# Copying a convolution out of PSUM earlier, and six narrow leading blocks in place of four, in a convolution + GELU MLP kernel

## Chip, cores, metric

One core of one Trainium2 chip. The metric is device time in microseconds (us), lower is better. The granted TensorE clock (the share of full speed that TensorE was given, 1.000 being all of it) is listed where it matters.

## The reference

`x` is [8, 4096, 192] fp32. A causal depthwise convolution of 7 taps (softmax-normalised weights, one set per group of 24 channels) feeds a two-layer MLP with exact GELU, 192 -> 2048 -> 192, over 32768 tokens:

```python
w = softmax(weight)                                   # [8, 7]
out[b, s, h, g] = sum_k w[h, k] * x_pad[b, s + k, h, g]   # 6 zeros ahead of each sequence
h = out @ w_in                                        # [32768, 2048]
y = (0.5 * h * (1 + erf(h / sqrt(2)))) @ w_out        # [32768, 192]
```

## The kernel before

Tokens go in blocks; each block holds a stretch of tokens of the first half of the batch on 64 partitions and the same stretch of the second half on the other 64. Per block, VectorE transposes x and does the convolution (21 operations: 7 taps for each of 3 channel groups), TensorE does the up-projection slice by slice into `hp` (PSUM), ScalarE does the GELU from `hp` to `gT`, and TensorE does the down projection of the block before, interleaved, into `ob` (PSUM), from where it is copied to `osb` and stored.

The first two blocks are an exception: TensorE does their convolution, with diagonal matrices. Their result sits in `ob` and is copied to `xc`, from where the up-projection reads it. For block 0 ScalarE copies, for block 1 VectorE (`conv_out`). Blocks are counted from 0: the third block is block 2.

```python
WS = [256] * 4 + [512] * ((HALF - 1024) // 512)   # block widths
PC = {0: 0, 1: 1}                                 # blocks whose convolution TensorE does
NA = 4                                            # blocks whose output ScalarE copies out of PSUM
...
def conv_out(n, p):                               # VectorE, L396
    v.wait_ge(S_PC, pce(n, p))                    # TensorE's convolution of group p is done
    b, o = CONVB[n][p]
    v.tensor_copy(xc[n % 2][:, p * TB : p * TB + WS[n]], ap(b, o, [[1024, 128], [1, WS[n]]])
    ).then_inc(S_PCE)
...
# VectorE's order for a block: 3 transposes (0-2), then 21 convolution steps (3-23).
# `side` puts other work ahead of a position: (block, position).
side = [((2, (4, 9, 14)[p]), conv_out, 1, p) for p in range(NP)]
for n in range(4, NB): ...                        # output copies (evac) of blocks 4.. by VectorE
...
# TensorE: block 1's up-projection waits for conv_out's S_PCE, then its first down projection
if n == 1 and a0 == 0 and a1 > 0:
    t.wait_ge(S_WOUT, 16)                         # w_out has landed
```

A slice of up-projection with its share of down projection takes TensorE 1.31 us and its GELU takes ScalarE 1.02 us, so in the steady state TensorE is the bound.

## Time and profile before

| | before |
|---|---|
| time, first three executions | 694.42, 694.45, 695.52 us |
| profiled execution | 695.67 us, span 693.8 us, granted clock 0.998 |
| busy in the span | PE 684.3, VectorE 554.3, ScalarE 531.4, GpSimd 44.6 us |
| TensorE idle | 9.5 us, nearly all before 30 us and after the last block |

In the profile's lines PE is TensorE (PEld its weight loads), DVE VectorE, ACT ScalarE, POOL GpSimd and SP SyncE. The span (first to last instruction) is 1.8 us shorter than the time of the same execution; times are compared with times and spans with spans. PE is 99% busy, so a change can gain only where TensorE stands still or runs at a lower clock. The prediction shows the lines.

### The profile page before, as it was taken

How to read it: one execution, taken by the hardware profiler on the slowest of the kernel's cores; microseconds unless marked ns; L12 is line 12 of the kernel's file. 1: busy time of each engine (PE TensorE's matmuls, PEld its weight loads, DVE VectorE, ACT ScalarE, POOL GpSimd, SP SyncE). 2: the span in 40 equal slices, each digit the busy share in tenths (PEclk: the TensorE clock that was granted, in tenths of full speed). 3: DMA queues.
4: the chain of work that ended last, by engine and by line, in shares of the span. 5: the costliest groups of instructions: out<-in, count | busy, mean ns of one | idle time of the engine just before them, and what ended most of it. 6: DMA issues, size and time to landing. Idle time of an engine off the chain costs nothing.

```text
span 693.8 us, 25405 instructions
## 1 busy us (share of the span) xinstructions
PE 684.3 (99%) x11556; PEld 502.5 (72%) x11556; DVE 554.3 (80%) x922; ACT 531.4 (77%) x532; POOL 44.6 (6%) x95
## 2 busy tenths in 40 slices
PE   8899999999999999999999999999999999999997
PEld 5696677777777777777777777777777777777777
DVE  6999677789777789778888777898877898777811
ACT  6589877777777777777777777777777777777771
POOL 7100000000000000000000000000000000000000
PEclk9999999999999999999999999999999999999999
DMA  9778453355543355543355543355543455521013
GB/s 200 161 167 186 104 119 87 85 124 138 138 112 87 90 126 137 138 105 89 88 132 137 138 101 86 90 138 137 135 99 78 102 138 137 134 50 33 17 47 94
DMA packets 23083, 78.16 MB, mean 113 GB/s; under 512 B 6976, under 2 KB 11200, under 8 KB 19136
## 3 DMA queue, kind: packets, MB, share of 16 engines
q1 hardware_dynamic: 18448, 72.26, 44.4%
q0 software_dynamic: 3792, 3.50, 2.9%
q8 instruction: 91, 1.49, 1.0%
q10 hardware_dynamic: 736, 0.78, 0.4%
q14 instruction: 16, 0.13, 0.1%
HBM read 52.92 MB, written 25.17 MB: 113 GB/s over the span
## 4 chain that ended last, share of the span: by engine, by line
PE 95%; DMA 2%; ACT 1%; DVE 1%; POOL 1%; issue 0%
PE ob L647 48%; PE hp L615 46%; DMA xin<-in_x_dram 2%; ACT gT L547 1%; DVE acc L443 0%; POOL xin L204 0%; DVE xT L413 0%; DVE acc L436 0%; POOL xTb L302 0%; ACT osb L194 0%; ACT L496 0%; DVE xc L396 0%; DVE osb L196 0%
## 5 line engine op out<-in xcount | busy, mean ns | idle before, releaser
L547 ACT ACTIVATE gT<-hp 128x1024 bf16<-128x1024 f32 x512 | 523.4, 1024 | 144.0 <-PE hp L615 144.0
L647 PEld LDWEIGHTS ob<-wout,gT 64*128 64x128 bf16 x8192 | 353.1, 94 | 115.2 <-PE ob L647 0.6
L647 PE MATMUL ob<-wout,gT 64*128 64x192 bf16 x8192 | 421.2, 243 | 0.1
L615 PE MATMUL hp<-xc,win 64*128 64x512 bf16 (+1 forms) x3264 | 416.7, 364 | 4.3 <-DVE xc L396 3.3
L443 DVE SCALAR_TENSOR_TENSOR acc<-xT,wcol,acc 128x512 f32<-128x512 f32 (+1 forms) x480 | 316.8, 722 | 0.0
L615 PEld LDWEIGHTS hp<-xc,win 64*128 64x128 bf16 x3264 | 150.3, 94 | 66.2 <-ACT gT L547 3.7
L196 DVE COPY osb<-ob 128x384 f32<-128x384 f32 x120 | 65.8, 548 | 128.8 <-PE ob L647 128.8
L443 DVE SCALAR_TENSOR_TENSOR xc<-xT,wcol,acc 128x512 bf16<-128x512 f32 (+1 forms) x96 | 64.5, 722 | 0.0
L413 DVE STREAM_TRANSPOSE xT<-xin 128x512 f32<-128x512 f32 (+1 forms) x102 | 61.0, 649 | 3.8 <-issue 2.1
L308 POOL COPY xT<-xT 128x558 f32<-128x558 f32 x32 | 20.9, 654 | 587.9 <-DVE xT L413 587.9
L436 DVE TENSOR_SCALAR acc<-xT,wcol 128x512 f32<-128x512 f32 (+1 forms) x96 | 55.4, 629 | 1.1
L291 POOL COPY xT<-xT 128x18 f32<-128x18 f32 x29 | 11.6, 398 | 4.9 <-DVE xc L396 4.9
L560 PE MATMUL hp<-warm 128*128 128x512 bf16 x16 | 6.0, 559 | 1.3 <-DVE warm L328 1.3
L576 PE MATMUL ob<-xTb,dg 64*64 64x256 bf16 x84 | 5.3, 271 | 0.3 <-ACT xTb L510 0.2
L560 PEld LDWEIGHTS hp<-warm 128*128 128x128 bf16 x16 | 2.1, 137 | 4.7 <-issue 3.2
L576 PEld LDWEIGHTS ob<-xTb,dg 64*64 64x64 bf16 x84 | 4.3, 107 | 1.5 <-ACT xTb L510 0.7
L204 POOL DMA_DIRECT2D xin<-in_x_dram x10 | 5.1, 514 | 0.0
L258 POOL DMA_DIRECT2D win<-in_moe_w_in_dram x6 | 3.9, 657 | 0.0
L194 ACT ACTIVATE osb<-ob 128x384 f32<-128x384 f32 x8 | 3.9, 484 | 0.0
L373 DVE COPY win<-win 64x768 bf16<-64x768 bf16 (+1 forms) x6 | 3.2, 526 | 0.3
L510 ACT ACTIVATE xTb<-xT 128x256 bf16<-128x256 f32 x3 | 1.1, 417 | 2.7 <-DVE xT L413 2.7
L302 POOL CAST xTb<-xT 128x186 bf16<-128x186 f32 x6 | 2.4, 404 | 2.4 <-DVE xT L413 2.4
(29 smaller groups left out, 14.1 us busy)
## 6 DMA issues: line engine op xcount, KB each, us to landing
xin<-in_x_dram SPq DMA_DIRECT2D x120, 380.0 KB, 6.6
out_dram<-osb SPq DMA_DIRECT2D x116, 192.0 KB, 3.1
out_dram<-osb SPq DMA_DIRECT2D x40, 48.0 KB, 1.9
xin<-in_x_dram POOLq DMA_DIRECT2D x10, 188.0 KB, 5.8
wout<-in_moe_w_out_dram POOLq DMA_DIRECT2D x1, 768.0 KB, 10.2
xin<-in_x_dram SPq DMA_DIRECT2D x4, 188.0 KB, 4.1
win<-in_moe_w_in_dram POOLq DMA_DIRECT2D x4, 96.0 KB, 4.3
win<-in_moe_w_in_dram POOLq DMA_DIRECT2D x2, 192.0 KB, 4.8
```

The lines of the kernel that those rows point to most:

```text
L196: e.tensor_copy(dst, src).then_inc(S_EV)
L204: e.dma_start(ap(xin[n % NX], 32 * q * (TB // 32 * D), [[TB // 32 * D, 32], [1, mb * D - 32]],), ap(xt, off, [[mb * D, 32], [1, mb * D - 3 ...
L291: g.tensor_copy(dst, ap(xT[(n - 1) % 2], WS[n - 1] + 31, [[NP * XW, 128], [XW, NP], [32, HB]],),).then_inc(S_HALO)
L308: g.tensor_copy(ap(t, 1, [[NP * tw, 128], [tw, NP], [32, HB], [1, 31]]), ap(t, WS[n], [[NP * tw, 128], [tw, NP], [32, HB], [1, 31]]),).the ...
L413: v.transpose(ap(xT[n % 2], p * XW + HL, [[NP * XW, 128], [1, w]]), ap(xin[n % NX], 64 * p, [[TB // 32 * D, 128], [D, w // 32], [1, 32]],) ...
L436: ins = v.tensor_scalar(a, src, wk, None, ALU.mult)
L443: ins = v.scalar_tensor_tensor(dst, src, wk, a, op0=ALU.mult, op1=ALU.add)
L547: a.activation(out=ap(gT[n % 2], i * c * 2 * w, dst), in_=ap(hp[u % 2], 0, src), func=AF.Gelu,).then_inc(S_GELU)
L560: t.matmul(hp[1][:, 0:512], warm[:, 0:128], warm[:, :])
L576: ins = t.matmul(b[r, o : o + w], dg[r, d0 : d0 + 64], xTb[PC[n]][r, x0 : x0 + w], start=(k == KS - 1), stop=(k == 0), tile_position=(64 * ...
L615: ins = t.matmul(hp[u % 2][:, hf * TB + cc * w : hf * TB + cc * w + w], win[r, p * F + wcols(hf, f0) : p * F + wcols(hf, f0) + 128], xc[n ...
L647: ins = t.matmul(ob[gg % 2][:, 512 * sub : 512 * sub + C], gT[m % 2][r, c0 : c0 + 128], wout[r, CH[i] * C : (CH[i] + 1) * C], start=(ph == ...
```

## The change

The intent: block 1's convolution should leave PSUM before block 2's transposes and most of block 2's convolution steps get in its way, and VectorE, pressed harder early on, should get easier early blocks. So the three copies move from positions 4, 9, 14 of block 2 to 0, 3, 5; and two more narrow blocks lead, whose outputs ScalarE copies.

```diff
-    WS = [256] * 4 + [512] * ((HALF - 1024) // 512)
+    WS = [256] * 6 + [512] * ((HALF - 1536) // 512)
-    NA = 4
+    NA = 6
-            side = [((2, (4, 9, 14)[p]), conv_out, 1, p) for p in range(NP)]
+            side = [((2, (0, 3, 5)[p]), conv_out, 1, p) for p in range(NP)]
-            for n in range(4, NB):
+            for n in range(NA, NB):
```

The first copy thus precedes block 2's transposes (position 0), the second follows them directly (3), the third comes two convolution steps later (5).

## The prediction

> **What bounds the kernel now.** I read the page first, then the waits between 16 and 30 us, the timeline of the first 110 us, and last the table of windows. The chain that ended last says which engine sets the end:

> ```profile
> ## 4 chain that ended last, share of the span: by engine, by line
> PE 95%; DMA 2%; ACT 1%; DVE 1%; POOL 1%; issue 0%
> ```

> TensorE carries 95% of the chain, and from 30 us to the last block it is 100% busy in every window. So nothing done for another engine after 30 us can gain anything; only an idle TensorE can give time back, and it idles in the first 30 us. The waits of 16 to 30 us name where (total us, times, longest us):

> ```profile
> PE hp L615 <- DVE xc L396: 3.3, 2, 1.8
> DVE xT L413 <- DMA xin<-in_x_dram: 1.5, 1, 1.5
> ```

> L396 is exactly what the change moves: VectorE copying block 1's convolution, which TensorE made in PSUM, to `xc`. The timeline (start us, duration us, engine, line) shows how late that copy is:

> ```profile
> 15.04 0.95 PE L576 MATMUL ob<-xTb,dg 64*64 64x256 bf16 x14
> 16.68 0.95 PE L576 MATMUL ob<-xTb,dg 64*64 64x256 bf16 x14
> 17.03 1.10 DVE L413 STREAM_TRANSPOSE xT<-xin 128x256 f32<-128x256 f32 x3 [1.51 <-DMA xin<-in_x_dram]
> 18.33 0.95 PE L576 MATMUL ob<-xTb,dg 64*64 64x256 bf16 x14
> 18.91 0.41 DVE L396 CAST xc<-ob 128x256 bf16<-128x256 f32 x1
> 19.21 0.83 PE L615 MATMUL hp<-xc,win 64*128 64x256 bf16 x12
> 20.95 0.41 DVE L396 CAST xc<-ob 128x256 bf16<-128x256 f32 x1
> 21.51 0.39 PE L615 MATMUL hp<-xc,win 64*128 64x256 bf16 x4 [1.47 <-DVE xc L396]
> 23.26 0.41 DVE L396 CAST xc<-ob 128x256 bf16<-128x256 f32 x1
> 23.73 1.03 PE L615 MATMUL hp<-xc,win 64*128 64x256 bf16 x8 [1.83 <-DVE xc L396]
> 25.52 1.35 PE L615 MATMUL hp<-xc,win 64*128 64x256 bf16 x12
> 27.37 0.81 PE L615 MATMUL hp<-xc,win 64*128 64x256 bf16 x12
> ```

> The three convolution parts are ready where the L576 groups end, at 16.0, 17.65 and 19.3 us, but copied at 18.91, 20.95 and 23.26, because the copies stand among block 2's convolution steps. TensorE, free at 20.04, stalls twice. It pays again afterwards (window; span; busy us of PE, PEld, DVE, ACT, POOL; granted clock; DMA share; GB/s):

> ```profile
> 9.53:12.95 3.42, 2.80 (x44) 1.62 (x39) 1.86 (x4) 2.33 (x4) 3.33 (x6) 1.00 1.04 243
> 19.77:23.19 3.42, 0.66 (x10) 0.14 (x4) 3.42 (x10) 1.02 (x1) 0.00 (x0) 1.00 0.74 185
> 23.19:26.60 3.41, 2.87 (x32) 2.22 (x34) 3.41 (x10) 1.02 (x1) 0.41 (x1) 0.50 0.59 150
> ```

> After a stretch with 0.66 us of work in 3.42 the clock is granted at 0.50 for the next 3.41 us. Stretches with 2.80 us of work did not cost it.

> [...] the first 256-wide TENSOR_SCALAR of block 2 took 0.83 us beside a GpSimd copy where its neighbours took 0.30. [...]

> **The change part by part.**

> *Move of the copies.* The first goes ahead of the transposes: ready at 16.0, it runs at about 16.05 to 16.46, inside the 1.51 us that VectorE waits for x until 17.03. It costs nothing. The second goes after the three transposes, 18.15 to 18.56 (ready 17.65). Then two TENSOR_SCALARs, one stretched by GpSimd (0.83 + 0.30), and the third copy at about 19.7 to 20.1 (ready 19.3). TensorE is free at 20.04, reaches the third part about 0.2 us later, and so does not stall. Block 1's first up-projection slice (12 matmuls, 0.65 us at full clock) ends near 20.7.

> *The next wait.* TensorE then waits for `w_out`:

> ```profile
> 11.38 1.21 POOL L317 DMA_DIRECT2D wout<-in_moe_w_out_dram  x1
> wout<-in_moe_w_out_dram POOLq DMA_DIRECT2D x1, 768.0 KB, 10.2
> ```

> 11.38 + 10.2 = 21.6 us. Before, that was hidden behind the late copies; now TensorE idles from 20.7 to 21.65. [...] Then 12 matmuls of the down projection (half of the 0.96 us that they took at half clock: 0.50), a slice of up-projection (0.65), 16 matmuls (0.66), and the third slice starts at 21.70 + 0.50 + 0.65 + 0.66 = 23.5, where before it started at 27.53 on the chain. Gain here: 4.0 us. The stalls give 3.3 - 0.95 = 2.35 of it, the clock about 1.6.

> *Six blocks of 256.* Two 256-blocks take the place of one 512-block; the work is the same. A slice with its share of down projection takes 1.315 us in 256-blocks (36.72 to 55.13 in 14 slices), 1.307 in 512-blocks: 16 slices x 0.008 = 0.13 us lost. ScalarE gets 4 more evictions at 0.48 us; 8 GELUs at 1.02 plus 2 x 0.48 = 9.1 us per block, against TensorE's 10.5, so nothing shows. The passage from the last 256-block to the first 512-block, where ScalarE sets the pace (16 GELUs in 15.95 us for TensorE's 15.7), moves from block 4 to block 6 and costs the same.

> Sum: 4.0 - 0.13 = about 3.85 us gained against the profiled execution.

> **Can VectorE keep up when TensorE is 4 us ahead?** This is what the second part is for. Before, block 4 and 5's convolutions end and block 4's first matmul comes at:

> ```profile
> 50.59 2.07 DVE L443 SCALAR_TENSOR_TENSOR xc<-xT,wcol,acc 128x512 bf16<-128x512 f32 x3
> 56.94 0.81 PE L615 MATMUL hp<-xc,win 64*128 64x512 bf16 x6
> 66.11 2.07 DVE L443 SCALAR_TENSOR_TENSOR xc<-xT,wcol,acc 128x512 bf16<-128x512 f32 x3
> ```

> With TensorE at 53.0 there, a 512-wide block 4 ready at 52.3 would have 0.7 us in hand. With 256-blocks VectorE needs 9.5 us per block against 10.5: block 2, ready at 27.63 before, loses its first copy (0.41) from the sequence and is ready at about 27.2; blocks 3, 4, 5 at 36.7, 46.2, 55.7. They are wanted at 32.0, 42.5, 53.0, 63.5 (36.06 - 4.0, and 10.5 more each). The first 512-block (15.6 us) is ready at 71.3 and wanted at 74.0: 2.7 us in hand. Block 7: 86.9 against 90.0. Old block 6, which starts at the same token as new block 7, began at 93.8; 93.8 - 90.0 = 3.8 confirms the sum. From there on TensorE is the bound as now.

> **Rivals.** (1) `w_out` lands later. By the landing records in the trace 15 of its 16 parts are there by 20.7 us and the last at 21.6, so the arrival is not firm; every us later costs one, and at 2 us later the clock could fall too (another 1.5), for 693 to 694. Against it: nothing that loads before it changes. Were it in time, the limit is another 0.95 us of gain: 690. (2) The 2.7 us at block 6 is used up, because the loads of x, queued behind stores, come late, or VectorE is slowed by GpSimd. Its load, 2.6 us after block 3 began before (49.16 against 46.6), would be issued near 45.1 and land by 52 (6.6 us in the page), wanted at 55.7; so against. Were it so, 1 to 2 us return: 693. (3) The timed executions don't hold the half-clock stretch. The profiled execution took 695.67 us, timed ones 694.42, 694.45 and 695.52. The 1.1 us between the two groups is close to the clock's 1.6[...], so the median may already be without it. Then the gain against the median is about 4.0 - 0.13 - 1.1 = 2.7, for 691.7; if profiling merely adds a us, it is 3.85, for 690.6.

> **Range and chances.** I weigh the two readings of (3) about 60 to 40 and add a little for (1): 691.4 us, which is 3 us or 0.44% less. Low end 690.2 (full gain, earlier `w_out`), high end 692.7 (`w_out` a us late). A change of 2% is 13.9 us; TensorE's idle time in the whole span is 693.8 - 684.3 = 9.5, so faster by 2% is next to impossible, and slower needs a stall that no view suggests: 0.01 each.

> **What would show it.** In the new profile: the three copies at L396 at about 16.1, 18.2 and 19.7 us; no wait of `hp` on `xc` there, but an idle TensorE of about 1 us ending near 21.6; granted clock 1.00 from 20 to 30 us; the third slice of block 1 near 23.5; block 6's first 512-wide matmul near 74 without a wait on VectorE; span near 690. I am wrong if the clock still falls to 0.50, if TensorE waits for VectorE at block 6, or if the copies stretch well beyond 0.41 us.

The sum came to 4.0 - 0.13 = about 3.85 us against the profiled execution. But about 1.6 of the 4.0 supposes that the clock stays at 1.00, and that was the author's guess. So is the fall of the clock if `w_out` came 2 us later, by likeness to the stretch with 0.66 us of work in 3.42.

## The result, and the profile after

The changed kernel took 692.07 us (median of 4, 691.64 to 692.22), the kernel before 694.91 (median of 4, 694.42 to 695.52): ratio 0.9958, 95% interval 0.994 to 0.9975. In a later session of five rounds it was 0.9945 (0.9933 to 0.9958). So: within 2%, and faster by about half a per cent.

The waits of the changed kernel between 10 and 30 us (total us, times, longest). No line has `hp` waiting on VectorE's copy to `xc` (L396) any more; this stands in its place:

```profile
PE ob L647 <- DMA wout<-in_moe_w_out_dram: 1.1, 1, 1.1
```

The timeline of the changed kernel (start us, duration us, engine, line):

```profile
16.27 0.42 DVE L396 CAST xc<-ob 128x256 bf16<-128x256 f32 x1 [0.51 <-PE ob L576]
17.08 1.10 DVE L413 STREAM_TRANSPOSE xT<-xin 128x256 f32<-128x256 f32 x3 [0.39 <-DMA xin<-in_x_dram]
18.10 0.39 DVE L396 CAST xc<-ob 128x256 bf16<-128x256 f32 x1
19.45 1.48 PE L615 MATMUL hp<-xc,win 64*128 64x256 bf16 x24
19.56 0.42 DVE L396 CAST xc<-ob 128x256 bf16<-128x256 f32 x1 [0.26 <-PE ob L576]
22.00 0.67 PE L647 MATMUL ob<-wout,gT 64*128 64x192 bf16 x12 [1.07 <-DMA wout<-in_moe_w_out_dram]
22.50 0.82 PE L615 MATMUL hp<-xc,win 64*128 64x256 bf16 x12
23.82 0.82 PE L615 MATMUL hp<-xc,win 64*128 64x256 bf16 x12
```

The first copy now fills part of VectorE's wait for x. The 24 matmuls from 19.45 on are block 0's last slice and block 1's first, in one piece: the two stalls of 1.47 and 1.83 us are gone. TensorE then stands for 1.07 us until `w_out` has landed. In the chain of the changed kernel, which is read as what released what, that load now covers the stretch where before the transposes, VectorE's convolution steps and its copies stood:

```profile
8.61 3.01 POOL xin L204 x6
11.62 10.33 DMA wout<-in_moe_w_out_dram
22.00 0.67 PE ob L647 x12
```

The windows of the changed kernel (span; busy us of PE, PEld, DVE, ACT, POOL; granted clock; DMA share; GB/s), around the wait for `w_out`; they are cut at whole multiples of 3.413 us after this execution's first clock record (4.98 us), the spacing of the clock's changes that e3 gives:

```profile
18.63:22.04 3.41, 2.34 (x41) 1.75 (x42) 3.15 (x9) 2.75 (x3) 0.54 (x2) 1.00 1.28 256
22.04:25.46 3.42, 3.35 (x70) 2.99 (x72) 3.42 (x10) 2.02 (x3) 0.00 (x0) 1.00 0.32 68
```

With 2.34 us of work in 3.41 the clock was kept: 1.00 in both. The third slice of block 1 starts at 23.82 where before, in the same view, it started at 27.37: 3.55 us gained. The lead is kept to the end almost whole: the last stretch of down projection starts at 675.48 instead of 678.91.

### The profile page after: what moved, and what is told of

It is laid out like the page before. It is cut to its first block, busy times and chain, and to the rows that moved or that the text cites. A ratio compares the mean times of both kernels' runs of the same rounds, so it can differ in the third digit from the quotient of the medians. Undisturbed runs are those within 1.5% of the kernel's fastest.

```text
span 690.5 us, 25644 instructions
## 1 busy us (share of the span) xinstructions
PE 682.3 (99%) x11652; PEld 506.3 (73%) x11652; DVE 555.7 (80%) x942; ACT 532.0 (77%) x536; POOL 45.1 (7%) x97
## 4 chain that ended last, share of the span: by engine, by line
PE 95%; DMA 2%; ACT 1%; POOL 1%; issue 0%; DVE 0%
PE ob L647 48%; PE hp L615 46%; DMA wout<-in_moe_w_out_dram 1%; ACT gT L547 1%; DMA xin<-in_x_dram 1%; POOL xin L204 0%; POOL xTb L302 0%; ACT osb L194 0%; ACT L496 0%; DVE osb L196 0%; DVE xT L413 0%
## 5 line engine op out<-in xcount | busy, mean ns | idle before, releaser
L615 PE MATMUL hp<-xc,win 64*128 64x512 bf16 (+1 forms) x3360 | 415.5, 358 | 1.0 <-ACT gT L547 0.7
L443 DVE SCALAR_TENSOR_TENSOR acc<-xT,wcol,acc 128x512 f32<-128x512 f32 (+1 forms) x495 | 318.7, 710 | 0.0
L615 PEld LDWEIGHTS hp<-xc,win 64*128 64x128 bf16 x3360 | 154.6, 94 | 61.0 <-ACT gT L547 1.9
L196 DVE COPY osb<-ob 128x384 f32<-128x384 f32 x116 | 63.9, 551 | 124.2 <-PE ob L647 124.2
L443 DVE SCALAR_TENSOR_TENSOR xc<-xT,wcol,acc 128x512 bf16<-128x512 f32 (+1 forms) x99 | 65.1, 713 | 0.0
L413 DVE STREAM_TRANSPOSE xT<-xin 128x512 f32<-128x512 f32 (+1 forms) x105 | 61.3, 635 | 2.9 <-issue 2.1
L308 POOL COPY xT<-xT 128x558 f32<-128x558 f32 x33 | 21.5, 652 | 587.5 <-DVE xT L413 587.5
L576 PE MATMUL ob<-xTb,dg 64*64 64x256 bf16 x84 | 5.3, 271 | 1.1 <-ACT xTb L510 1.0
L576 PEld LDWEIGHTS ob<-xTb,dg 64*64 64x64 bf16 x84 | 4.3, 106 | 2.3 <-ACT xTb L510 1.5
L194 ACT ACTIVATE osb<-ob 128x384 f32<-128x384 f32 x12 | 5.8, 486 | 0.0
## 6 DMA issues: line engine op xcount, KB each, us to landing
wout<-in_moe_w_out_dram POOLq DMA_DIRECT2D x1, 768.0 KB, 10.3
```

Source lines behind the costliest of these rows:

```text
L194: e.activation(out=dst, in_=src, func=AF.Copy).then_inc(S_EVA)
L196: e.tensor_copy(dst, src).then_inc(S_EV)
L308: g.tensor_copy(ap(t, 1, [[NP * tw, 128], [tw, NP], [32, HB], [1, 31]]), ap(t, WS[n], [[NP * tw, 128], [tw, NP], [32, HB], [1, 31]]),).the ...
L413: v.transpose(ap(xT[n % 2], p * XW + HL, [[NP * XW, 128], [1, w]]), ap(xin[n % NX], 64 * p, [[TB // 32 * D, 128], [D, w // 32], [1, 32]],) ...
L443: ins = v.scalar_tensor_tensor(dst, src, wk, a, op0=ALU.mult, op1=ALU.add)
L576: ins = t.matmul(b[r, o : o + w], dg[r, d0 : d0 + 64], xTb[PC[n]][r, x0 : x0 + w], start=(k == KS - 1), stop=(k == 0), tile_position=(64 * ...
```

## The experiments

Eleven runs, all correct: nine new kernels, the changed kernel again (e5) and e8 again (e11). Those of one table ran on one chip in the same rounds, five or six executions each.

| first session | median us | ratio to before, 95% | granted clock |
|---|---|---|---|
| before (11 runs) | 695.85 | 1 | 0.995 to 1.000 |
| e1 copies moved, four blocks | 692.20 | 0.9948 (0.9935 to 0.9962) | 0.999 to 1.000 |
| e2 six blocks, copies late | 695.64 | 1.0000 (0.9984 to 1.0016) | 0.995 to 1.000 |
| e3 before, stalls filled | 694.88 | 0.9988 (0.9974 to 1.0002) | 0.999 to 1.000 |
| e4 changed, block 3's x after `w_out` | 690.93 | 0.9932 (0.9918 to 0.9945) | 0.999 to 1.000 |

**e1, the moved copies alone.** Edit, against the kernel before:

```diff
-            side = [((2, (4, 9, 14)[p]), conv_out, 1, p) for p in range(NP)]
+            side = [((2, (0, 3, 5)[p]), conv_out, 1, p) for p in range(NP)]
```

> Only the earlier copies, four 256-blocks as before. My theory: the whole gain is made before 30 us, so this keeps it and loses nothing to the extra 256-blocks: 691.9 us against 692.07 of the changed kernel, ratio to before about 0.9955. VectorE finishes block 4's convolution near 52.5 us, TensorE wants it near 53.3, so no wait on VectorE. Rival: with TensorE over 3 us earlier, a 512-wide block 4 is ready too late; then hp waits on xc near 53 us and this run is 0.5 to 2 us slower than the changed kernel.

Measured: 692.20, span of the profiled execution 689.9. The changed kernel did not run in these rounds, but its ratios to the kernel before, 0.9958 and 0.9945 in e5, lie on both sides of this 0.9948: the whole gain is in this one line. In its timeline, VectorE's last convolution steps of block 4 (now 512 wide) and TensorE's first matmuls of that block:

```profile
49.98 2.06 DVE L443 SCALAR_TENSOR_TENSOR xc<-xT,wcol,acc 128x512 bf16<-128x512 f32 x3
53.02 0.81 PE L615 MATMUL hp<-xc,win 64*128 64x512 bf16 x6
```

Ready at 49.98 + 2.06 = 52.04, wanted at 53.02: 0.98 us in hand, no wait. The rival falls: with TensorE this early, four narrow blocks were enough.

**e2, the six blocks alone.** Edit: the changed kernel with positions (4, 9, 14) for the copies.

> Only the six 256-blocks evicted by ScalarE, copies as late as before. My theory: no gain, about 0.15 us slower than before (16 slices x 0.008 us), hp waits on xc 3.3 us at 21 to 24 us as before. Rival: relieving VectorE early is worth something itself: 1 us or more faster than before.

Measured: ratio 1.0000; the interval of 0.16% (1.1 us) holds my 0.15 us of loss as well as none. Its waits show the old stalls (2.9 us of `hp` on `xc`). Relief for VectorE is worth nothing that these runs resolve while TensorE waits on the order of VectorE's work.

**e3, the stalls filled with idle matmuls.** Edit, against the kernel before; the target is a PSUM bank that nothing uses at that time, and the results are never read:

```diff
+                def idle_fill(k):
+                    for _ in range(k):
+                        t.matmul(ob[1][:, 512:1024], warm[:, 0:128], warm[:, :])
+                if (n, i) == (1, 0):
+                    idle_fill(6)          # ahead of the wait for the second copy
...
                         if n in PC and i == 0 and cc == 0 and p == NP - 1:
+                            if n == 1:
+                                idle_fill(7)      # ahead of the wait for the third copy
```

> The kernel before with 13 idle matmuls (512 wide, zeros, 0.22 us each, into an unused PSUM bank) put into TensorE's two stalls of 1.47 and 1.83 us; nothing waits for them. My theory: the stalls stay, the clock no longer falls to 0.50 at 23 us, so about 1.5 us faster than those executions of before that have the fall (694 of 695.4). Rival: the half clock is hidden behind other waits, and nothing is gained: 695.4.

Measured: 694.88 (mean 694.89), each of its five executions at a clock of 0.999 or 1.000. The group of six idle matmuls took 1.47 us, the group of seven 1.68, so 0.21 for one more. Its windows, in the view explained above:

```profile
19.80:23.20 3.40, 3.40 (x21) 1.23 (x18) 3.40 (x10) 1.02 (x1) 0.06 (x1) 1.00 0.56 145
23.20:26.60 3.40, 3.34 (x67) 2.92 (x68) 3.40 (x10) 2.33 (x3) 0.36 (x1) 1.00 0.69 177
```

The useful work is as late as before: the third copy begins 4.36 us after the first (18.32 and 22.68 us; before 4.35, 18.91 and 23.26, since everything in this execution is about 0.6 us earlier). But the clock stays at 1.00. The interval of the ratio does not quite exclude 1: before itself has two kinds of executions, and both are in it. Over the three sessions it ran 31 times with the clock listed:

| before, by mean granted clock | executions | mean us | range |
|---|---|---|---|
| 0.995 to 0.998 | 24 | 696.16 | 695.25 to 697.08 |
| 0.999 to 1.000 | 7 | 694.32 | 693.39 to 695.50 |

So executions that lost the clock took 1.84 us more, close to 1.7, half a stretch of 3.41 us (an estimate: in e6's chain twelve matmuls of up-projection took 1.28 us while the clock was at 0.50 and 0.65 at 1.00). That alone is a correlation; e3 makes it a cause: idle work alone, put where TensorE stood, removes the lost clock in all five executions, and its mean is 1.3 us below the 696.16. It is 0.6 us above the 694.32. The profiles give the same size: from the start of block 1's last convolution part to its third slice TensorE took 2.26 us in e3 (23.20 to 25.46) and 3.64 before (23.73 to 27.37). So the lost clock itself is worth 1.3 to 1.4 us; what makes up the rest of the 1.84 is not shown. In e3's profile TensorE has one extra pause of 0.53 us at 48.66 us that follows no wait; what it is stays open.

```profile
19.41:22.82 3.41, 1.13 (x16) 0.55 (x14) 3.41 (x10) 1.18 (x2) 0.00 (x0) 1.00 0.90 216
```

What parts before's two kinds of executions is not shown, since none of the kind with the full clock was profiled.

**e4, `w_out` with less company.** Edit, against the changed kernel:

```diff
-            load(g, 3, SW[3], S_XG[3])
             for n in range(2, NB):
                 halo(n)
+                if n == 2:
+                    g.wait_ge(S_WOUT, 16)
+                    load(g, 3, SW[3], S_XG[3])
```

> The changed kernel, but GpSimd issues block 3's load of x only after w_out has landed, so that w_out has the DMA engines more to itself from 15 us. My theory: the 1.07 us wait of TensorE on w_out is the bound now, so w_out lands up to 1 us earlier and the time falls by as much: 691.1 us. Rival: w_out's arrival [...] lands at 21.9 as now, and the time stays at 692.1; or block 3's x comes late (wanted by VectorE at 27.3) and it is slower.

A clause of the rival, on what sets the arrival of `w_out`, is cut, since no run shows it.

Measured: 690.93, 1.27 us below e1 of the same rounds, which is the changed kernel with four narrow blocks. Its chain, from what released the first down projection:

```profile
11.54 9.34 DMA wout<-in_moe_w_out_dram
```

and its waits between 10 and 60 us:

```profile
PE ob L649 <- DMA wout<-in_moe_w_out_dram: 0.3, 1, 0.3
```

`w_out` takes 9.34 us instead of 10.33 and the wait for it shrinks from 1.1 to 0.3 us: the time follows. That wait was the bound of the changed kernel's start. From 16.40 to 19.80 us DMA moved 161 GB/s here and 207 in the changed kernel. That `w_out` was faster because block 3's x no longer shared the DMA engines with it is argued and not shown: over all profiles but e6's it took 9.6 to 10.9 us with that load beside it and 9.3 to 10.1 with the load held back (e4, e7, e9, e10), so single profiles overlap. That the edit makes the run faster is clear: none of its five executions is as slow as any of e1's.

| second session | median us | ratio to before, 95% |
|---|---|---|
| before (9 runs) | 695.80 | 1 |
| e5 changed kernel again | 692.22 | 0.9945 (0.9933 to 0.9958) |
| e6 changed, two narrow blocks | 697.81 | 1.0027 (1.0014 to 1.0039) |
| e7 e4 with four narrow blocks | 691.53 | 0.9934 (0.9922 to 0.9947) |
| e8 changed, a slice ahead of the wait | 691.04 | 0.9927 (0.9914 to 0.9941) |

**e5, the changed kernel again** (no edit).

> The changed kernel unaltered, as the yardstick of this chip and these rounds: 692.1 us, granted clock 0.999 to 1.000 in every execution, while executions of before split into slow ones with a clock of 0.995 to 0.998 (near 695.9) and fast ones at 0.999 or 1.000 (near 694.4). Rival: the clock column of before has nothing to do with its time.

Measured: 692.22, all five at 0.999 or 1.000. Of before's nine executions, seven at 0.995 or 0.997 took 695.70 to 697.08, two at 0.999 and 1.000 took 693.97 and 695.50. The second of these lies next to the slow kind, so the clock is the larger part of the scatter and not all of it.

**e6, two narrow blocks.** Edit, against the changed kernel:

```diff
-    WS = [256] * 6 + [512] * ((HALF - 1536) // 512)
+    WS = [256] * 2 + [512] * ((HALF - 512) // 512)
-    NA = 6
+    NA = 2
```

> The changed kernel with two 256-blocks in place of six: block 2 is 512 wide. Theory: the leading 256-blocks are there so that VectorE, starting at 17 us, has each block's convolution ready before TensorE wants it. Block 2's takes 15.6 + 0.8 us, so it is ready near 33.5 where TensorE wants it near 32: hp waits on xc about 1.5 us and the run is 1 to 1.5 us slower than the changed kernel (693.3). Rival: block width early on makes no difference; 691.9.

Measured: 697.81, 5.6 us slower than e5, four times what I expected, and by another mechanism. Its timeline:

```profile
21.53 1.90 DVE L413 STREAM_TRANSPOSE xT<-xin 128x512 f32<-128x512 f32 x3 [4.79 <-DMA xin<-in_x_dram]
23.35 0.39 DVE L396 CAST xc<-ob 128x256 bf16<-128x256 f32 x1
23.88 0.59 PE L615 MATMUL hp<-xc,win 64*128 64x256 bf16 x4 [3.57 <-DVE xc L396]
24.74 0.41 DVE L396 CAST xc<-ob 128x256 bf16<-128x256 f32 x1
25.20 1.04 PE L615 MATMUL hp<-xc,win 64*128 64x256 bf16 x8 [0.73 <-DVE xc L396]
```

A block of 512 needs 380 KB of x in each of its four transfers instead of 188, block 2's x lands at 21.5 us, and the second and third copies, which stand behind the transposes in VectorE's order, wait with them. TensorE stalls for 4.3 us in two waits, and the clock falls again (0.50 from 23.94 to 30.77 us by the trace's clock records, twice 3.41 us: the first 3.41 held 2.69 us of matmul and 0.50 followed, while the 3.41 us at 0.50 in before, with 2.87, and in e2, with 2.81, were followed by 1.00). So the early positions are only early when x is; and here the narrow third block mattered for its load, not for VectorE's convolution. The wait that I had expected at block 2, ready at 37.47 and begun at 38.68, did not come.

**e7, four narrow blocks with the early `w_out`.** Edit: e4's edit and e1's block widths.

> Earlier copies, four 256-blocks, and block 3's load of x issued after w_out has landed. Theory: TensorE reaches block 4 at 52.3 us, VectorE has it ready at 52.0, so this is the margin's edge: 690.9 us as with six blocks, give or take 0.3. If six blocks were needed for this start, hp waits on xc near 52 us and it is slower than 690.9 by that wait.

Measured: 691.53, 0.69 below e5 and 0.6 above what I expected. The margin is indeed used up in its profile:

```profile
50.46 2.06 DVE L445 SCALAR_TENSOR_TENSOR xc<-xT,wcol,acc 128x512 bf16<-128x512 f32 x3
52.63 0.36 PEld L617 LDWEIGHTS hp<-xc,win 64*128 64x128 bf16 x6 [0.28 <-issue]
52.66 0.82 PE L617 MATMUL hp<-xc,win 64*128 64x512 bf16 x6
```

VectorE is ready at 52.52, the first weights of block 4 load at 52.63 after 0.28 us in which nothing else is shown to hold them. That is the edge: a wait of at most 0.3 us, which is half of the miss; the rest may be the session, since e4, from which I took 690.9, ran on another chip.

**e8, a slice of up-projection ahead of the wait.** Edit, against the changed kernel (weights of block 1's eight slices, by which the down projection is spread over them; the first slice now gets none, and with it the wait for `w_out` moves behind the second slice):

```diff
-            share = {1: [3, 4, 4, 4, 4, 4, 4, 4]}
+            share = {1: [0, 4, 4, 4, 5, 5, 5, 5]}
```

> The changed kernel, but TensorE does its second up-projection slice of block 1 before it waits for w_out (the down projection it skipped is spread over the later slices). Theory: the slice of 0.65 us runs inside the 1.07 us wait, so the time falls by about 0.6 us, to 691.4, though w_out lands no earlier. Rival: the later slices are then bound by ScalarE or by the wait for the GELU, and nothing is gained: 692.1.

Measured: 691.04, 1.2 us below e5 instead of 0.6. Its timeline:

```profile
21.22 0.83 PE L615 MATMUL hp<-xc,win 64*128 64x256 bf16 x12 [0.47 <-ACT gT L547]
21.89 0.82 PE L647 MATMUL ob<-wout,gT 64*128 64x192 bf16 x16
```

No wait on `w_out` is left; 0.47 us of waiting for a GELU took its place, since the extra slice needs the PSUM buffer that ScalarE is still reading. Against the wait on `w_out` of 0.93 us in e5's profile that is 0.5 us gained (0.6 against the 1.07 of the first profile). The rest has a candidate in the same profile: over 10 to 90 us the pauses of `ob` on `ob` (0.3 us where the down projection passes from its first to its second half and needs the first complete) were two in e5 and are one here, as that passage now falls at a slice boundary; that would be 0.3 us. The remaining 0.3 to 0.4 is not traced.

| third session | median us | ratio to before, 95% |
|---|---|---|
| before (11 runs) | 695.86 | 1 |
| e9 e4 and e8 together, six narrow blocks | 691.32 | 0.9936 (0.9922 to 0.9950) |
| e10 the same, four narrow blocks | 690.98 | 0.9933 (0.9919 to 0.9947) |
| e11 e8 again | 691.38 | 0.9939 (0.9923 to 0.9954) |

**e9, both remedies.** Edit: e4's and e8's.

> Both remedies for the wait on w_out at once (block 3's x issued after it has landed, and a slice of up-projection ahead of the wait), six 256-blocks. Theory: each alone gave about 1.0 to 1.2 us; with w_out landing near 20.9 the slice of 0.65 us now pushes the down projection to about 21.6, so little is added: 690.6 to 690.9 us. Rival: they add up: 690.0.

Measured: 691.32, no better than e11 of the same rounds. They do not add up: in its profile the extra slice still starts at 21.18, held 0.47 us by the GELU, and nobody waits for `w_out`. Nor did `w_out` come earlier here: it took 10.1 us, and 9.6 in e11's profile, so this pair does not test what an earlier `w_out` would be worth.

**e10, the same with four narrow blocks.**

> The same with four 256-blocks. Theory: VectorE has block 4 ready at 52.5 us and TensorE would want it near 52.3 or earlier, so TensorE waits for VectorE at block 4 and the run is 0.2 to 0.8 us slower than with six blocks. Rival: the number of 256-blocks makes no difference within 0.15 us.

Measured: 690.98, 0.34 below e9, so not slower. Its timeline:

```profile
49.98 2.07 DVE L445 SCALAR_TENSOR_TENSOR xc<-xT,wcol,acc 128x512 bf16<-128x512 f32 x3
52.20 0.81 PE L617 MATMUL hp<-xc,win 64*128 64x512 bf16 x6
```

Ready at 52.05, wanted at 52.20: just in time. Six blocks were not needed here either. The sign agrees with the 0.13 us of my estimate for the two extra narrow blocks, but such a difference is at the limit of what five or six executions resolve.

**e11, e8 again** (no edit).

> The version with the slice ahead of the wait alone, again, as yardstick of these rounds: 691.0 us.

Measured: 691.38, 0.34 above its first session; so small differences are compared only inside a session here. By that rule e10, e4 and e8 are each about 1.2 us or more better than the changed kernel or its four-block form e1 (e10 by way of e11); none is clearly the best of the three, and all beat both kernels.

## Why the prediction was right

The time, 691.4 us with a range of 690.2 to 692.7, met 692.07. By its steps:

- *The copies at about 16.05, 18.15 and 19.7 us, at 0.41 each*: right; 16.27, 18.10 and 19.56, at 0.42, 0.39 and 0.42. e1 shows that this move is the whole gain, e2 that the rest of the change is none.
- *No stall on `xc`, and an idle TensorE of about 1 us until `w_out`*: right; 1.07 us. e4 and e8 show that this wait is the new bound: take it away from either side and over 1 us more comes.
- *`w_out` at 21.6 us*: 0.3 too early; 21.95. x landed later in this execution (6.74 us against 6.46 on the chains), `w_out` was issued 0.24 us later (11.62 against 11.38) and took 10.33 us against 10.2.
- *4.0 us at the third slice*: mis-sized; 3.55. Of the 0.45, 0.30 is the later start on `w_out` (22.00 us, I had 21.70). The other 0.15 is a mistake in the prediction: I built 23.5 from starts in the timeline, and took before's start (27.53) from the chain, which counts from the end of the work ahead; the timeline has 27.37 for the same slice. One view for both would have given 27.37 - 23.5 = 3.87. The measured parts: the stalls 3.30 - 1.07 = 2.23 (predicted 2.35); the work between, which took 4.03 us before and 2.47 after, 1.56 (predicted about 1.6 for the clock, of which e3 confirms 1.4); less 0.24 by which this execution was later from the start.
- *0.13 us lost to the narrow blocks*: the size fits; the lead falls from 3.55 at the third slice to 3.43 at the block that starts at token 2048 (90.38 against 93.81 us), and stays 3.43 to the last down projection. No set of times resolves so little.
- *The clock stays at 1.00*: right, and e3 shows that its fall had cost time of its own. That it would stay was a guess: the least work that had been followed by the full clock until then was 2.80 us in 3.42. Here it was 2.34 in 3.41.
- *TensorE 100% busy in every window from 30 us on*: nearly; it is idle for 0.2 us of the 630 us from 30 to 660.
- *VectorE 2.7 us ahead at the first wide block (rival 2)*: right; ready at 71.43, wanted at 74.43, 3.0 us. That the six blocks are there to make it keep up was too much, and the prediction's own 0.7 us in hand for a 512-wide block 4 said so: four leave 0.98 us (e1), and were enough even at 0.15 (e10).
- *Rival 3, that the median of before might be without the half clock*: this is what put the prediction at 691.4 instead of 690.6, and the clocks listed later support it: executions of before at full clock average 694.32, next to the first two (694.42, 694.45), while the profiled one (695.67, clock 0.998) sits with the others. Against executions at full clock the gain of the changed kernel is 2.1 us, against the others 3.9 (694.32 and 696.16 less 692.25, the mean of e5). The weighing of 60 to 40 was for the reading that held. What was left, 692.07 instead of the 691.7 of that reading, is about the size of the later `w_out`. That the gain of 3 us also fits the measured difference of medians, 2.84, is in part luck: it depends on how many of before's four executions lost the clock. In the later session, where seven of nine did, the same difference is 3.58.
- *The copies at 0.41 us, not well beyond*: right, also beside GpSimd. Before's three copies could not show this, since none ran beside a copy of GpSimd. In the changed kernel the second one did (18.10 to 18.49 us, GpSimd's from 18.24 to 18.89) and took 0.39 us, no longer than the others.
- *One TENSOR_SCALAR stretched by GpSimd, 0.83 + 0.30*: the two took 0.89 us together in the changed kernel. The first took 0.63 us, 0.48 of them beside GpSimd's copy of 0.65 us, and the second 0.34; before's first took 0.83 us beside the whole of that copy, and its next two 0.34 each. Why they took longer is not shown.

The timeline rows from which "ready" and "wanted" of the changed kernel are read:

```profile
69.36 2.07 DVE L443 SCALAR_TENSOR_TENSOR xc<-xT,wcol,acc 128x512 bf16<-128x512 f32 x3
74.43 0.81 PE L615 MATMUL hp<-xc,win 64*128 64x512 bf16 x6
```

## What to carry to other kernels

Where the bound engine waits for a short operation of another engine, look at the order of that engine's instructions before its load: three copies of 0.4 us, placed among work that nobody was waiting for yet, cost over 2 us, and placing them where their inputs are ready was the whole gain. Then ask what the bound engine waits for next, because the gain ends there; here it was a weight load that had been hidden, and holding another load back, or putting work ahead of the wait, was worth about another 1.2 us (0.7 in e7). And when executions of one kernel scatter by more than the effect, sort them by granted clock before comparing (before: 696.16 and 694.32 us).
